# Another written order of all operations for a gated linear attention fused with an expert-style MLP

## The chip, the cores and the metric

One core of a Trainium2 chip runs the whole program. The metric is the device time of one execution in microseconds, and the median of several runs is compared. Profiles are of one execution.

## The reference

For 4 batches of 8 heads, 768 steps and a head width of 40, the first half is a recurrent attention with input, forget and output gates. The second half is an MLP from 320 to 2,048 to 320 on all 3,072 tokens.

```python
for t in range(S):
    m_new = np.maximum(f_gate[:, :, t] + m, i_gate[:, :, t])
    f_stab = np.exp(f_gate[:, :, t] + m - m_new)
    i_stab = np.exp(i_gate[:, :, t] - m_new)
    C = f_stab * C + i_stab * outer(vt, kt)
    n = f_stab * n + i_stab * kt
    y[:, :, t] = sigmoid(o_gate) * (C @ qt) / np.maximum(np.abs(n @ qt), 1.0)
x = y.transpose(0, 2, 1, 3).reshape(B * S, H * D)
h = x @ w_in
sp = np.maximum(h, 0.0) + np.log1p(np.exp(-np.abs(h)))
out = (h * erf(sp)) @ w_out
```

## The kernel before, in words

The sequence is cut into 12 chunks of 64 steps (`NC`), and within a chunk everything is done for two pairs of batches (`r` = 0, 1). A chunk of attention consists of a gate block for every second chunk (`gate_block`: the scan at L303 and what follows to L327), decay factors (`dm`: for chunks 0 and 1 by a matmul at L444 from the tiles `lt`, L340, and `xd`, L350 and L348, with an exponential at L449; later through DRAM, L456), scores on TensorE (L507), the masked product on VectorE (L562), the state and key products (L516, L521) and the value matmuls (L530), the normalisation (L593 to L607) and the state update (L614, L616). The result is transposed on TensorE (L389 to L393) and split into a rounded half and a remainder, `xh` (L402, ACT) and `xl` (L406, VectorE).

The weights of the MLP arrive as 64-bit words whose two 32-bit halves are put together on the core: L624 and L635 on VectorE, L630 on ACT. Those of `w_in` are then split into halves `wh` (L645, L683, ACT) and `wl` (L649, L687, VectorE). They come in four parts of 512 columns.

The MLP of a chunk has 4 groups (`mlp(g)`, 48 in all), each of 512 of the 2,048 middle columns. A group's first matmuls (L748) write two or four `h` tiles, for which PSUM has two buffers. ACT empties them (L759). Then follow softplus (L768), erf (L772), the product (L776), a split (L786 or L788 and L792), and the output matmuls (L812 for the first four groups, L814 to L817 for the others). Exponential, softplus and erf lie in three different tables of ACT, and a change of table is an instruction of its own (L876).

Every piece is added to a plan with its engine and its dependencies. Nothing decides the order at run time: `ORDER`, a list of 1,595 numbers, gives the order in which all operations are written, and each engine, SP's DMA queue included, works through its own in that order. A negative number -n writes n filler matmuls (L873), which compute nothing and keep TensorE busy during the start. A table load is written wherever the next ACT operation needs another table than the one loaded.

```python
for i in order:
    if i < 0:
        stay(-i)
        continue
    o = self.ops[i]
    if o.table and loaded not in o.table:
        loaded = o.table[0]
        load(loaded)
    o.fn()
```

Of the kernel before, what the change touches and what calls it, by code (L numbers as in the profile page):

```python
# [33 lines left out]
class Plan:  # L34
# [60 lines left out]
    1, 4, 0, 3, 5, 7, 9, 11, 12, 6, 13, 2, 14, 15, 16, 8, 17, 33, 27, 32, 34, 36, 35, 20, 19, 31, 38, -1, 40, 28, 26, 29, 93,  # L95
    95, 349, 350, 351, 42, -2, 47, 94, 48, 49, 18, 67, 68, 99, 96, 10, 50, 59, 60, 25, 37, 30, 39, 52, 65, 23, 100, 101, 102,
    105, 107, 106, 108, 41, -2, 55, 44, 66, 72, 56, 109, 43, 24, 71, 354, 45, 46, 111, 112, 57, 74, 76, 58, 22, 69, 73, -1, 64,
    75, 70, 103, 104, 352, 353, 357, 97, 98, 51, 53, 135, 136, 137, 138, 63, 139, 110, 54, 140, 129, 130, 131, 132, 21, 169,
    171, 170, 133, 172, 61, 163, 358, 78, 83, 134, 86, 164, 84, 85, 221, 222, 165, 166, 62, 241, 157, 173, 174, 167, 168, 159,
    239, 240, 125, 127, 158, 160, 175, 199, 200, 161, 242, 88, 193, 77, 91, 201, 195, 205, 207, 223, 224, 225, 162, 273, 79,  # L100
    80, 81, 82, 87, 89, 274, 202, 203, 355, 371, 206, 141, 194, 142, 121, 92, 122, 275, 276, 90, 248, 226, 489, 208, 490, 491,
    204, 196, 249, 227, 356, 369, 113, 209, 250, 143, 197, 251, 361, 114, 372, 210, 115, 494, 149, 126, 128, 492, 457, 467,
    374, 198, 286, 287, 150, 123, 288, 373, 376, 230, 362, 363, 289, 176, 299, 493, 151, 231, 458, 459, 462, 124, 152, 495,
    117, 211, 116, 300, 118, 375, 119, 290, 252, 232, 243, 244, 380, 316, 317, 333, 120, 228, 366, 468, 370, 377, 291, 719,
    720, 378, 382, 212, 359, 364, 365, 721, 185, 384, 360, 496, 253, 145, 379, 392, 337, 233, 245, 389, 186, 724, 466, 368,
    146, 381, 177, 178, 153, 318, 154, 189, 229, 383, 190, 390, 391, 456, 394, 144, 301, 469, 472, 367, 191, 155, 147, 148,
    156, 246, 187, 385, 386, 387, 388, 460, 292, 498, 192, 397, 398, 188, 267, 319, 347, 217, 455, 218, 234, 343, 725, 393,
    395, 396, 268, 461, 474, 320, 277, 302, 235, 247, 181, 497, 399, 400, 278, 464, 475, 473, 236, 477, 465, 470, 334, 182,
    471, 981, 425, 479, 481, 482, 426, 213, 484, 321, 322, 219, 293, 261, 501, 401, 179, 605, 726, 511, 294, 254, 502, 402,
    427, 428, 183, 214, 595, 728, 303, 429, 215, 512, 265, 476, 438, 439, 478, 220, 412, 279, 184, 180, 266, 323, 259, 463,  # L110
    257, 335, 503, 271, 263, 280, 480, 488, 510, 485, 593, 509, 606, 258, 486, 237, 238, 216, 260, 324, 729, 264, 336, 487,
    499, 722, 504, 727, 262, 483, 338, 596, 272, 255, 256, 297, 430, 723, 513, 269, 270, 281, 516, 345, 304, 982, 305, 983,
    505, 295, 298, 500, 296, 325, 339, 340, 326, 327, 597, 440, 506, 431, 508, 986, 413, 306, 307, 329, 330, 414, 331, 519,
    284, 432, 403, 328, 514, 741, 525, 527, 532, 529, 282, 283, 530, 521, 522, 594, 515, 308, 309, 518, 285, 520, 441, 442,
    415, 416, 417, 418, 443, 341, 1243, 603, 523, 344, 524, 742, 312, 313, 310, 404, 405, 348, 526, 550, 551, 406, 576, 990,
    311, 528, 577, 314, 537, 538, 419, 598, 315, 407, 517, 507, 563, 564, 408, 731, 433, 533, 444, 536, 342, 1244, 531, 599,
    608, 740, 552, 553, 554, 607, 539, 540, 565, 732, 534, 535, 1245, 600, 602, 743, 746, 613, 615, 578, 420, 409, 619, 621,
    410, 411, 346, 421, 730, 604, 609, 626, 610, 623, 624, 601, 616, 612, 423, 541, 542, 445, 625, 543, 555, 566, 857, 858,
    859, 614, 617, 618, 611, 620, 424, 436, 579, 631, 632, 633, 640, 641, 642, 733, 736, 622, 634, 635, 630, 636, 652, 653,
    654, 984, 985, 1248, 673, 674, 675, 655, 748, 422, 656, 657, 734, 735, 446, 661, 662, 663, 739, 862, 679, 680, 681, 627,  # L120
    628, 434, 694, 695, 738, 696, 332, 1249, 867, 682, 683, 684, 437, 556, 637, 638, 639, 697, 698, 567, 749, 751, 699, 544,
    700, 701, 755, 658, 659, 660, 580, 664, 702, 545, 629, 451, 452, 453, 744, 745, 987, 703, 676, 435, 677, 678, 685, 752,
    757, 759, 762, 760, 643, 686, 447, 548, 549, 448, 557, 449, 750, 753, 754, 704, 705, 756, 546, 547, 788, 568, 569, 581,
    789, 790, 558, 570, 791, 792, 793, 559, 737, 761, 830, 831, 665, 832, 582, 836, 837, 838, 758, 571, 855, 839, 840, 841,
    687, 561, 809, 815, 562, 574, 988, 989, 810, 816, 811, 644, 450, 767, 868, 869, 872, 768, 817, 860, 861, 856, 766, 666,
    797, 747, 798, 560, 572, 769, 1246, 818, 819, 645, 646, 573, 763, 866, 874, 799, 864, 820, 1247, 764, 765, 873, 776, 777,
    778, 1003, 770, 771, 772, 647, 875, 583, 881, 1004, 1005, 584, 870, 1002, 1119, 575, 794, 795, 773, 774, 796, 775, 667,
    706, 877, 589, 833, 812, 590, 993, 994, 688, 834, 591, 454, 585, 586, 883, 587, 800, 835, 842, 813, 865, 650, 651, 671,
    888, 707, 843, 885, 886, 878, 814, 588, 648, 871, 1129, 1130, 863, 876, 879, 1120, 880, 649, 669, 991, 821, 914, 668, 670,
    690, 779, 689, 915, 916, 882, 708, 1131, 1134, 917, 918, 919, 935, 936, 937, 801, 672, 893, 894, 895, 709, 691, 938, 939,  # L130
    710, 940, 692, 693, 992, 592, 941, 715, 716, 780, 781, 802, 884, 956, 822, 995, 1008, 942, 943, 1010, 962, 887, 892, 957,
    958, 711, 782, 963, 964, 823, 920, 921, 922, 902, 903, 717, 1121, 712, 904, 889, 944, 945, 783, 946, 899, 786, 996, 997,
    900, 901, 1006, 713, 998, 824, 1000, 890, 1001, 896, 1250, 1255, 897, 898, 844, 803, 923, 924, 925, 947, 926, 804, 1128,
    1251, 1011, 825, 1017, 1256, 1007, 965, 966, 959, 960, 961, 891, 784, 1019, 1024, 1021, 1257, 1013, 905, 787, 785, 807,
    808, 1260, 805, 967, 968, 1014, 1022, 948, 1012, 999, 1015, 1016, 828, 1009, 927, 906, 806, 949, 1092, 1093, 1094, 1029,
    845, 829, 1030, 1031, 928, 1095, 1096, 1097, 826, 1018, 950, 951, 1050, 1098, 1020, 1051, 1099, 1052, 1100, 846, 714, 1252,
    1122, 907, 1035, 1036, 1037, 1025, 1026, 1028, 1038, 1039, 1135, 969, 1040, 1118, 1127, 1136, 1117, 1123, 851, 718, 1264,
    1265, 1056, 1124, 1126, 1381, 1057, 1058, 827, 847, 1053, 1054, 1055, 848, 849, 1059, 1060, 1061, 1023, 1101, 1102, 1103,
    929, 852, 970, 1382, 1032, 1125, 1071, 853, 1072, 1073, 1137, 930, 1143, 908, 1033, 1034, 1077, 909, 971, 1078, 1079, 1062,
    1063, 910, 1080, 1139, 1074, 1081, 912, 1027, 1145, 1253, 1147, 1150, 1148, 1140, 1075, 1076, 913, 1132, 1133, 1082, 1268,  # L140
    1254, 933, 934, 911, 954, 1138, 1104, 1105, 1106, 1141, 1142, 1064, 1083, 1041, 1144, 854, 972, 955, 977, 1262, 1149, 1176,
    1177, 1042, 1178, 931, 932, 1218, 1146, 1151, 1219, 1220, 1084, 978, 979, 1263, 980, 1224, 1225, 1226, 1043, 1155, 1156,
    952, 1197, 1157, 1065, 1198, 1152, 1199, 1044, 953, 1185, 1186, 1164, 1154, 1187, 1266, 1267, 1270, 1165, 1166, 973, 1383,
    1045, 974, 975, 1107, 1221, 1222, 1258, 1223, 1161, 1162, 1271, 1048, 1259, 1163, 1390, 1391, 1085, 1269, 1182, 1183, 1200,
    1201, 1184, 1202, 1066, 1153, 1273, 1158, 1159, 1160, 1227, 1228, 1229, 1049, 1275, 1276, 1179, 1180, 1086, 1279, 1181,
    1392, 1395, 1206, 1108, 1069, 1389, 976, 1203, 1167, 1207, 1204, 1070, 1379, 1281, 1286, 1283, 1188, 1189, 1046, 1047,
    1067, 1090, 1208, 1205, 1284, 1272, 1274, 1277, 1068, 1088, 1393, 1380, 1278, 1333, 1334, 1354, 1355, 1087, 1089, 1335,
    1280, 1357, 1358, 1261, 1387, 1356, 1359, 1291, 1292, 1293, 1282, 1287, 1288, 1388, 1360, 1361, 1168, 1362, 1290, 1339,
# [789 lines left out]
```

## Time and profile before

| | |
|---|---|
| median of 3 runs | 459.67 us (459.19 to 460.89) |
| span of the profiled execution | 456.7 us |
| TensorE busy | 445.6 us, 98% of the span |
| VectorE busy | 336.5 us, 74% |
| ACT busy | 328.5 us, 72% |
| mean granted TensorE clock | 0.996 |
| moved by DMA | 51.82 MB, mean 113 GB/s |

The span runs from the first to the last instruction of the profiled execution; a run's time has what lies around it too, so the two differ by some 3 us. Matmuls are pipelined and their ends are modelled, so a TensorE that is busy for a whole stretch is one that was never seen without a matmul under way. The profile lists a full float32 matmul twice. "Idle before" is the time that an engine stood still ahead of an instruction, with the one that ended the wait.

### The profile page before, as it was taken

How to read it: one execution, taken by the hardware profiler on the slowest of the kernel's cores; microseconds unless marked ns; L12 is line 12 of the kernel's file. 1: busy time of each engine (PE TensorE's matmuls, PEld its weight loads, DVE VectorE, ACT ScalarE, POOL GpSimd, SP SyncE). 2: the span in 40 equal slices, each digit the busy share in tenths (PEclk: the TensorE clock that was granted, in tenths of full speed). 3: DMA queues.
4: the chain of work that ended last, by engine and by line, in shares of the span. 5: the costliest groups of instructions: out<-in, count | busy, mean ns of one | idle time of the engine just before them, and what ended most of it. 6: DMA issues, size and time to landing. Idle time of an engine off the chain costs nothing.

```text
span 456.7 us, 14133 instructions
## 1 busy us (share of the span) xinstructions
PE 445.6 (98%) x6118; PEld 401.6 (88%) x6118; DVE 336.5 (74%) x657; ACT 328.5 (72%) x524; POOL 37.3 (8%) x62
## 2 busy tenths in 40 slices
PE   6979999999999999999999999999999999999996
PEld 4569988888999988989998998899898899999996
DVE  5899989799768766588468948776845869548762
ACT  4758999898976946855996984998445584773760
POOL 2000131003300220001021100001110000000000
PEclk9989999999999999999999999999999999999999
DMA  7889696836613430065405217342341100100011
GB/s 273 273 264 332 170 321 177 217 95 199 184 40 106 136 107 3 3 195 130 133 1 163 72 27 238 72 113 78 107 128 26 30 1 2 29 2 15 1 45 29
DMA packets 46831, 51.82 MB, mean 113 GB/s; under 512 B 27056, under 2 KB 31664, under 8 KB 46768
## 3 DMA queue, kind: packets, MB, share of 16 engines
q1 hardware_dynamic: 46768, 50.91, 38.2%
q8 instruction: 48, 0.79, 0.7%
q14 instruction: 15, 0.12, 0.1%
HBM read 46.77 MB, written 4.13 MB: 111 GB/s over the span
## 4 chain that ended last, share of the span: by engine, by line
PE 92%; DVE 3%; ACT 2%; DMA 1%; issue 1%; SPq 0%; DVEq 0%
PE h L748 40%; PE pob L816 11%; PE pob L814 11%; PE pob L817 11%; PE pa L530 3%; PE pa L507 3%; PE pa L516 3%; PE pa L812 2%; PE pob L812 2%; PE pa L521 2%; PE pa L389 2%; PE pa L444 1%; PE pob L873 1%; DMA eT<-gd 1%; DMA gt<-in_gates_dram 1%
## 5 line engine op out<-in xcount | busy, mean ns | idle before, releaser
L748 PE MATMUL h<-xh,wh 128*128 128x256 f32 (+1 forms) x768 | 201.4, 345 | 0.2 <-DVE hb L764 0.2
L748 PEld LDWEIGHTS h<-xh,wh 128*128 128x128 f32 x768 | 126.0, 190 | 14.1 <-DVE hb L764 0.5
L759 ACT ACTIVATE hb<-h 128x256 f32<-128x256 f32 (+1 forms) x160 | 66.7, 422 | 82.7 <-PE h L748 82.6
L748 PE MATMUL h<-xh,wl 128*128 128x256 f32 x384 | 108.5, 283 | 0.2 <-DVE wl L649 0.2
L816 PE MATMUL pob<-woh,gh 128*128 128x320 f32 x336 | 101.1, 313 | 0.0
L817 PE MATMUL pob<-wo,gh 128*128 128x320 f32 x336 | 100.1, 310 | 0.0
L764 DVE TENSOR_TENSOR hb<-h,hb 128x256 f32<-128x256 f32 x128 | 53.1, 420 | 45.8 <-ACT hb L759 45.2
L748 PEld LDWEIGHTS h<-xh,wl 128*128 128x128 f32 x384 | 72.9, 190 | 2.7 <-DVE wl L649 0.5
L876 ACT ACT_TABLE_LOAD x54 | 69.3, 1283 | 1.7 <-PEq L926 0.8
L776 DVE TENSOR_TENSOR n<-n,hb 128x1024 f32<-128x1024 f32 x48 | 58.6, 1227 | 14.8 <-ACT n L772 14.7
L817 PEld LDWEIGHTS pob<-wo,gh 128*128 128x128 f32 x336 | 63.2, 188 | 1.4
L816 PEld LDWEIGHTS pob<-woh,gh 128*128 128x128 f32 x336 | 63.2, 188 | 0.5
L814 PE MATMUL pob<-woh,gl 128*128 128x320 f32 x336 | 62.7, 312 | 0.0
L485 POOL TENSOR_SCALAR_AFFINE_SELECT dm<-dm 128x512 f32<-128x512 f32 (+1 forms) x40 | 34.0, 856 | 293.9 <-ACT dm L465 256.6
L792 DVE TENSOR_TENSOR gl<-n,gh 128x1024 fp32r<-128x1024 f32 x44 | 53.9, 1228 | 2.2 <-ACT gh L786 1.9
L814 PEld LDWEIGHTS pob<-woh,gl 128*128 128x128 f32 x336 | 53.5, 188 | 2.0
L768 ACT ACTIVATE n<-hb 128x1024 f32<-128x1024 f32 x48 | 49.3, 1058 | 1.6 <-DVE hb L764 1.3
L772 ACT ACTIVATE n<-n 128x1024 f32<-128x1024 f32 x48 | 49.6, 1054 | 0.2
L786 ACT ACTIVATE gh<-n 128x1024 fp32r<-128x1024 f32 x28 | 29.5, 1052 | 0.0
L406 DVE TENSOR_TENSOR xh<-pa,xh 128x384 fp32r<-128x384 f32 x24 | 13.3, 554 | 15.1 <-ACT xh L402 15.1
L562 DVE TENSOR_TENSOR dm<-pa,dm 128x512 f32<-128x512 f32 x24 | 16.5, 687 | 9.6 <-ACT xh L402 6.0
L530 PEld LDWEIGHTS pa<-kvo,dm 64*32 64x32 f32 x1536 | 16.7, 106 | 5.9 <-issue 5.0
(99 smaller groups left out, 469.6 us busy)
## 6 DMA issues: line engine op xcount, KB each, us to landing
qk<-in_qk_dram SPq DMA_DIRECT2D x24, 512.0 KB
kvo<-in_kvo_dram SPq DMA_DIRECT2D x24, 484.0 KB
eT<-gd SPq DMA_DIRECT2D x44, 128.0 KB
raw<-in_w_out_dram SPq DMA_DIRECT2D x16, 320.0 KB
dm<-gd SPq DMA_DIRECT2D x40, 128.0 KB
raw<-in_w_in_dram SPq DMA_DIRECT2D x8, 512.0 KB
out_dram<-o SPq DMA_DIRECT2D x48, 80.0 KB
raw<-in_w_in_dram SPq DMA_DIRECT2D x4, 256.0 KB
```

What stands on the lines that cost most here:

```text
L485: nc.gpsimd.affine_select(out=x, in_=x, pattern=[[0, H], [1, L]], compare_op=ALU.is_ge, fill=0.0, base=base, channel_multiplier=-1)
L748: nc.tensor.matmul(h[:, n * T:n * T + n_], w, m, start=(s == 0), stop=(s == len(ops) - 1))
L759: nc.scalar.activation(part(), G(f'h{i}')[:, T:2 * T] if wide else G(f'h{i}'), AF.Copy)
L764: nc.vector.tensor_tensor(part(), G(f'h{i}')[:, 0:T], part(), op=ALU.add)
L768: nc.scalar.activation(new('n0', [128, 1024], ('n0', g)), G('hb'), AF.Softplus)
L772: nc.scalar.activation(G('n0'), G('n0'), AF.Erf)
L776: nc.vector.tensor_tensor(G('n0'), G('n0'), G('hb'), op=ALU.mult)
L792: nc.vector.tensor_tensor(new('gl', [128, 1024], ('gl', g), F32R), G('n0'), G('gh').bitcast(F32), op=ALU.subtract)
L814: nc.tensor.matmul(acc(b), G('gl')[:, ts], woh[:, j], start=False, stop=(j == NFF - 1))
L816: nc.tensor.matmul(acc(b), G('gh')[:, ts], woh[:, j], start=(j == 0), stop=False)
L817: nc.tensor.matmul(acc(b), G('gh')[:, ts], t['wol', j], start=False, stop=False)
L876: plan.run(ORDER, lambda k: nc.scalar.preload_act_table_set(KIND[k]), stay)
```

## The change

The list `ORDER` is replaced by another permutation of the same operations. No operation, tile or buffer count is touched, and six filler matmuls are written in both, at other places.

```diff
 ORDER = [
-    1, 4, 0, 3, 5, 7, 9, 11, 12, 6, 13, 2, 14, 15, 16, 8, 17, 33, 27, 32, 34, 36, 35, 20, 19, 31, 38, -1, 40, 28, 26, 29, 93,
...
+    4, 135, 9, -2, 0, 12, 137, 5, 99, 8, 6, -1, 136, 2, 1, 3, -1, 138, 11, 7, 13, 139, 32, 31, 101, 14, 105, 15, 17, 349,
...
```

What it does is seen on the queues. First SP's DMA queue at the start of the program (`cst` are the constants, `gt` the gates, `raw` weights, `kvo` and `qk` the attention's inputs), before:

```order
L223 DMA cst<-in_consts_dram 128x12
L293 DMA gt<-in_gates_dram 128x2x128
L439 DMA kvo<-in_kvo_dram 128x968
L435 DMA qk<-in_qk_dram 128x2x512
L439 DMA kvo<-in_kvo_dram 128x968
L657 DMA raw<-in_w_in_dram 128x1024
```

and in the changed kernel:

```order
L657 DMA raw<-in_w_in_dram 128x1024
L223 DMA cst<-in_consts_dram 128x12
L293 DMA gt<-in_gates_dram 128x2x128
L657 DMA raw<-in_w_in_dram 128x1024
L439 DMA kvo<-in_kvo_dram 128x968
L435 DMA qk<-in_qk_dram 128x2x512
L673 DMA raw<-in_w_in_dram 64x1024 x2
```

Two blocks of first-layer weights and the tail block now stand among the first transfers, one of them ahead of the constants.

Second, VectorE at the start, up to the gate scan (L303), as the difference of the two:

```order
 L934 UNCONDITIONAL_BRANCH
+L272 MEMSET state_71 128x328
 L252 TENSOR_TENSOR sel<-cst 128x1
 L253 TENSOR_TENSOR sel<-cst 128x1
 L254 TENSOR_TENSOR sel<-sel 128x1
 L255 TENSOR_SCALAR sel<-sel 128x1
-L272 MEMSET state_71 128x328
+L268 TENSOR_SCALAR heads_of<-cst,sel 128x8
 L259 TENSOR_SCALAR sel<-block,sel 128x4
+L624 TENSOR_SCALAR raw<-raw 128x512
+L635 SCALAR_TENSOR_TENSOR raw<-raw 128x512
 L303 SCALAR_TENSOR_TENSOR m<-gt,m 128x128
```

The decoding of the first weight block now stands ahead of the gate scan, and the head mask (`heads_of`) moves ahead of it as well.

Third, TensorE ahead of the first expert matmul (L748; `pa` are the attention's tiles in PSUM, `pob` the fillers'). Before, this stands there, and behind its last row nine more of the same value block (L521 and L530) and then L748:

```order
L507 MATMUL pa<-qk 64x64 x32
L873 MATMUL pob_77<-ident 128x512
L360 MATMUL pa<-ident,x 128x32 x2
L389 MATMUL pa<-ident,kvo 128x128 x2
L392 MATMUL pa<-ident,kvo 64x128
L393 MATMUL pa<-ident,kvo 64x128
L516 MATMUL pa<-state_72,qe 64x41 x16
```

and in the changed kernel:

```order
L530 MATMUL pa<-kvo,dm 32x41 x32
L873 MATMUL pob_77<-ident 128x512 x2
L389 MATMUL pa<-ident,kvo 128x128 x2
L392 MATMUL pa<-ident,kvo 64x128
L393 MATMUL pa<-ident,kvo 64x128
L389 MATMUL pa<-ident,kvo 128x128 x2
L392 MATMUL pa<-ident,kvo 64x128
L393 MATMUL pa<-ident,kvo 64x128
L507 MATMUL pa<-qk 64x64 x16
L360 MATMUL pa<-ident,x 128x32 x2
L748 MATMUL h<-xh,wh 128x256 x2
```

One of chunk 1's two score blocks and its first state and value block (L516, L521, L530) now stand behind the first expert matmuls. Further on, all engines' rows are shuffled in the same way, and ACT has 66 table loads (L876) where it had 54.

## Rows read from the trace of the kernel before

**Rows 1.** The page's first part: busy us (share of the span) xinstructions of each engine.
```profile
PE 445.6 (98%) x6118; PEld 401.6 (88%) x6118; DVE 336.5 (74%) x657; ACT 328.5 (72%) x524; POOL 37.3 (8%) x62
```

**Rows 2.** Table by stretches: length; busy (x) of PE, PEld, DVE, ACT, POOL; PEclk, DMA share, GB/s.
```profile
core 0: us, PE busy (x) PEld busy (x) DVE busy (x) ACT busy (x) POOL busy (x), PEclk, DMA share, GB/s
...
10.00:20.00 10.00, 9.85 (x272) 5.80 (x273) 8.03 (x22) 7.73 (x23) 0.00 (x0) 1.00 1.03 340
20.00:30.00 10.00, 7.23 (x194) 4.65 (x196) 9.50 (x20) 6.61 (x14) 0.00 (x0) 1.00 0.73 202
30.00:40.00 10.00, 9.77 (x155) 9.00 (x158) 9.49 (x21) 6.08 (x11) 0.00 (x0) 0.83 1.03 333
...
140.00:160.00 20.00, 20.00 (x378) 19.28 (x377) 15.58 (x34) 17.60 (x25) 2.71 (x4) 1.00 0.43 123
160.00:180.00 20.00, 20.00 (x262) 17.61 (x261) 11.95 (x26) 10.02 (x22) 2.71 (x4) 1.00 0.20 63
```

**Rows 3.** Timeline, 27 to 41 us, PE and DVE: start, length, engine, line, operation.
```profile
27.47 0.65 PE L530 MATMUL pa<-kvo,dm 64*32 64x41 f32 x46
...
29.34 0.56 DVE L406 TENSOR_TENSOR xh<-pa,xh 128x384 fp32r<-128x384 f32 x1
...
29.95 0.38 PE L530 MATMUL pa<-kvo,dm 64*32 64x41 f32 x18 [1.83 <-issue]
...
30.26 0.51 PE L748 MATMUL h<-xh,wh 128*128 128x256 f32 x2
...
33.89 0.58 PE L748 MATMUL h<-xh,wl 128*128 128x256 f32 x1 [0.23 <-DVE wl L649]
...
38.73 0.68 PE L516 MATMUL pa<-state,qe 40*64 40x41 f32 x32
...
40.53 0.51 PE L748 MATMUL h<-xh,wh 128*128 128x256 f32 x2
```

**Rows 4.** Timeline, 0 to 20 us, the same columns.
```profile
0.80 0.40 SPq L223 DMA_DIRECT2D cst<-in_consts_dram  x1
...
2.55 0.16 DVE L252 TENSOR_TENSOR sel<-cst 128x1 f32<-128x1 f32 x1 [2.55 <-DMA cst<-in_consts_dram]
...
3.90 0.48 DVE L303 TENSOR_TENSOR_SCAN m<-gt,m 128x128 f32<-128x128 f32 x1 [0.32 <-DMA gt<-in_gates_dram]
...
6.72 1.06 ACT L340 ACTIVATE lt<-x,sel 128x64 f32<-128x64 f32 x4 [2.54 <-DVE x L327]
...
7.18 0.69 DVE L350 TENSOR_TENSOR xd<-x,heads_of 128x512 f32<-128x512 f32 x1
...
8.02 1.96 PE L444 MATMUL pa<-xd,lt 128*128 128x512 f32 x4
...
9.15 0.60 ACT L449 ACTIVATE dm<-pa 128x512 f32<-128x512 f32 x1 [1.37 <-PE pa L444]
...
10.21 2.00 ACT L348 ACTIVATE xd<-x,heads_of 128x64 f32<-128x64 f32 x8
...
19.07 0.81 PE L530 MATMUL pa<-kvo,dm 64*32 64x41 f32 x64
```

**Rows 5.** VectorE's groups by form: busy us, mean ns of one, idle before.
```profile
L562 DVE TENSOR_TENSOR dm<-pa,dm 128x512 f32<-128x512 f32 x24 | 16.5, 687 | 9.6 <-ACT xh L402 6.0
...
L478 DVE TENSOR_TENSOR qe<-qk,eT 104x512 f32<-104x512 f32 x22 | 16.0, 725 | 0.0
...
L635 DVE SCALAR_TENSOR_TENSOR raw<-raw 128x512 int32<-128x512 int32 x10 | 6.9, 690 | 0.6
...
L649 DVE TENSOR_TENSOR wl<-raw,wh 128x512 fp32r<-128x512 f32 x8 | 5.5, 682 | 0.5 <-ACT wh L645 0.5
...
L624 DVE TENSOR_SCALAR raw<-raw 128x512 int32<-128x512 int32 x10 | 4.2, 422 | 0.0
...
L687 DVE TENSOR_TENSOR wh<-raw,wh 64x512 fp32r<-64x512 f32 x4 | 2.7, 687 | 0.1
```

**Rows 6.** The chain that ended last, one group of sixteen L748.
```profile
82.83 1.91 PE h L748 x16
```

**Rows 7.** ACT's groups: table loads, busy us, mean ns of one, idle before.
```profile
L876 ACT ACT_TABLE_LOAD x54 | 69.3, 1283 | 1.7 <-PEq L926 0.8
```

140 rows, old and new, of the table ORDER are left out of this document.

## The prediction, made before the changed kernel was run

> **What bounds the kernel now.** Read the busy shares first: TensorE is busy for 445.6 of 456.7 us [rows 1], so only some 11 us of the span can be won without shortening its work, and the change shortens none of it. The table by stretches says where the 11 us lie. TensorE is busy for 9.85 of the ten microseconds from 10 to 20, for 7.23 from 20 to 30 and 9.77 from 30 to 40, there with a granted clock of 0.83, and from 140 on for 20.00 of 20 [rows 2]. From about 34 us to the last matmul the kernel is a TensorE queue that never runs dry, and any order that keeps it fed ends when the work ends. What an order can still change is how early the queue fills, and whether it runs dry later.
>
> The timeline shows how it fills. The first expert matmul (L748) starts at 30.26. Before it the queue waits 1.83 us inside the value matmuls of chunk 1, which the profile puts down to issue, but VectorE's last half of the activations (L406) ends at 29.90, so without that wait the first expert matmul would have waited for VectorE to about the same moment [rows 3]. Three microseconds on, a matmul waits for a weight half (L649, at 33.89) [rows 3]. VectorE is busy for 9.50 of 10 us from 20 to 30 and 9.49 from 30 to 40 [rows 2]. So the start is bound by VectorE's queue and by the order in which inputs land, and everything after it by TensorE.
>
> **The change, part by part.** All 1,595 operations stay, as do the six filler matmuls; three things move.
>
> *Constants behind a weight block.* The first transfer is now 512 KB of w_in. The constants were issued at 0.80 and were there at 2.55 [rows 4]. At the 340 GB/s of the busy stretch [rows 2] the block takes 1.54 us. If the constants queue fully behind it they come 1.54 late, if they run beside it, not at all; I take 1.2, nearer to the queue, since the sixteen DMA engines are fully busy at that rate (share 1.03 [rows 2]): 3.75. Ahead of the gate scan (L303, 3.90 before [rows 4]) VectorE now also decodes that block: L624 0.42 and L635 0.69 [rows 5]. The scan starts at about 3.75 + 1.1 for the small constants + 1.1 = 5.95, 2.05 later. The head mask, once between scan and decay factors (about 0.3 us), now stands ahead, so the decay factors (L350, 7.18 before) come 1.75 late at 8.95, and the first decay matmul (8.02 before [rows 4]) at 9.8.
>
> *ACT's own queue.* Two blocks of L340 (1.06 each [rows 4]) and the 0.3 us exponential now stand ahead of the first decay exponential (9.15 before): it runs from 11.2 to 11.8, 2.05 late [rows 4]. Scores then run to 12.55, and the first value matmuls end near 14.2, about 1.2 late. From there the new order gains: the second half of ACT's decay factors (2.00 us, [rows 4]) ends at 14.5, the scores of the second pair wait for VectorE to free their buffer (gate block 2.3, one L624 0.42, normalisation 1.0 after 13.35, so 17.3), and its value matmuls run at about 19.7 against 19.07 before [rows 4]. That leaves the start 0.6 us late, not early.
>
> *What stands ahead of the first expert matmul.* Before, both score blocks of chunk 1 and one whole value block stood there, and on VectorE the operations that go with them. Now one score block does. VectorE after the normalisation (22.2) has two halves, two weight pieces and a decode between: L649, L687, L635, L406, L624, L406, 3.6 us, to 25.85. The first expert matmul then starts at about 26.4, 3.85 us earlier than 30.26. TensorE has done less by then: a value block with its state product (38.73 to 40.53, 1.80 us [rows 3]) and a score block (0.65). Net: +1.4 us.
>
> *The next VectorE point.* The value block of chunk 1's first pair now needs VectorE's L562 24 instructions later. Those are four L635, three L624 and two each of L649, L687, L478 and L562, 9.6 us by their means [rows 5], and nine of 0.2 to 0.5, 3.5 us: 13.1. At the pace of 30 to 40 us (21 in 9.49 us [rows 2]) 24 take 10.8. I take 12.8, nearer to the sum of the forms, because these are the long ones. So 38.65, with small waits 38.85, and the block ends at 39.65. TensorE, with two 1.91 us groups [rows 6], the other block and two groups more, would be there at 37.6 and waits. Before, the same block ended at 40.53 [rows 3], with one 1.91 us group fewer and one set of transposes (0.78) more done. Gain: 0.88 + 1.91 - 0.78 = **2.0 us**. Ends: if VectorE keeps the faster pace and the constants do not queue, TensorE sets the end here and the gain is about 4.5; if the clock falls as before and VectorE is held up by it, 0.5.
>
> *Twelve more table loads.* ACT's order holds 66 where 54 stood, at 1,283 ns [rows 7]: 15.4 us of ACT. ACT is busy for 328.5 of 456.7 us [rows 1], so the cover is its own idle time of 128 us, and the sum takes nothing. The worst stretch is from the first group of experts of chunk 3 to the last of chunk 5 (about 120 to 200 us), where 13 loads stand instead of 7. From 140 to 180 ACT is busy for 17.60 and 10.02 of 20 [rows 2], 12.4 us idle against 7.7 us of added loads. If that cover were gone, each load would cost TensorE up to 1.283 us, because only two PSUM buffers hold its results until ACT has emptied them.
> What a load costs is shown by its row: 1,283 ns, and 1.7 us of idle time ahead of all 54 together [rows 7]. The Trainium skill (ScalarE: Activation LUTs, What ACT_TABLE_LOAD costs) adds a drain of about 1,380 ns to every switch, 2.66 us in all; by it the added loads would be an estimated 32 us of ACT, and six of them 16 us, more than the idle time of 140 to 180. By that rule the trace disagrees: no such drain stands beside the loads here as idle time.
>
> **Sum.** 456.7 - 2.0 = 454.7 us of span. The median of the runs, 459.67, lies 3.0 above that span, which I take as unchanged: **457.7 us**, 0.43% faster. A measurement of this kernel can tell about 0.5%, 2.3 us, from no change.
>
> **The rivals.**
> *The gain is larger.* VectorE is not the limit at the value block, and the clock never falls. For it: two stretches with TensorE's loss, 2.77 us from 20 to 30 and some 1.7 from the clock [rows 2], need not come again. Against it: VectorE is already busy for 9.5 of 10 there, and the new order asks 24 of its instructions first. Gain 4.5: 455.2.
> *The clock takes it back.* The new order leaves TensorE little to do from 14.2 to 17.4, with one decay matmul between. Before, the granted clock of 30 to 40 was 0.83, that is 3.4 of the ten microseconds at 1.2 GHz and 1.7 us lost, after the wait that ended at 29.95 [rows 2, 3]. If it drops at the new gap, score and value blocks and the two fillers that stand ahead of the transposes run at 1.2 GHz and all that follows is late by about 1.7 us: 459.4.
> *Slower: the loads starve TensorE.* Place: 120 to 200 us, six added loads. It decides once four of the added loads fall where ACT has no idle time: 5.1 us, more than the 2.0 won and the 2.3 of the measurement. For it: two result buffers only, and ACT's share in that stretch goes to about 90%. Against it: from 160 to 180 ACT is idle half the time, and in the crowded stretches of the kernel before TensorE still never stopped. 457.7 + 5.1: 462.8.
> *It is no different.* That the table changes nothing is excluded, since the rows of every queue move; that the start only changes places, with the first weights early and the gates late, is the lower end of the forecast.
>
> **How the numbers follow.** Forecast 0.50, spread from 456.3 to 458.9, with 0.4 of it past the 0.5% line at 457.4; larger gain 0.20; clock 0.20, inside the line; loads 0.10, of which 0.02 stay inside it. Faster: 0.20 + 0.20 = 0.40. Slower: 0.08. Within: 0.52. The range runs from the larger gain, 455.2, to a drop of the clock with one uncovered load besides, 459.4 + 1.0 = 460.4; the loads and the far end of the larger gain are left out.
>
> **What would show it.** Right: the first L748 at 26 to 27 us, the constants at 3.3 to 4.1, a TensorE wait of about a microsecond for L562 before the value block at 39, TensorE at 20.00 of 20 from 60 us on, 66 loads, and the last matmul near 450.3. Wrong: a first L748 after 28.5, a granted clock below 1 between 15 and 30, L759 with its two buffers as what TensorE waits for between 120 and 200, or a wait between the last expert group and the last output matmuls, where 60 matmuls now stand and 72 did. A first L748 before 25 would speak for the larger gain.

## The result, and the profile after

The changed kernel took 465.35 us (median of 20 runs, 460.01 to 467.58), the kernel before 459.88 (20 runs, 458.25 to 462.51): a ratio of 1.0092, 95% interval 1.0067 to 1.0117. The ratio leaves out the three slowest of the twenty runs, which count as slow; the quotient of the two medians over all runs is 1.0119. The forecast of 457.7 is wrong in sign, and 465.35 lies beyond its range, which ended at 460.4. The profiled execution after took 461.46 us with a span of 459.7, so it is one of the faster ones: sixteen of the twenty runs took longer than 463 us. A second profile (464.19 us) follows below.

From the page of the changed kernel, the busy shares and ScalarE's table loads:

```profile
PE 446.5 (97%) x6118; PEld 401.9 (87%) x6118; DVE 333.1 (72%) x657; ACT 344.1 (75%) x536; POOL 37.9 (8%) x62
...
L876 ACT ACT_TABLE_LOAD x66 | 84.7, 1283 | 1.9 <-PEq L926 0.8
```

Against [rows 1] and [rows 7], TensorE's work is the same to 0.9 us, and the twelve added loads stand there with 15.4 us of ScalarE and 1.9 us of idle time ahead of all 66 together. The span is 3.0 us longer, so TensorE stands or is slowed somewhere. The table by stretches of the changed kernel (columns as in [rows 2]) says where:

```profile
10.00:20.00 10.00, 6.82 (x155) 3.87 (x159) 7.47 (x20) 8.06 (x25) 0.00 (x0) 0.83 0.97 251
20.00:30.00 10.00, 9.16 (x187) 6.01 (x177) 8.82 (x19) 5.96 (x11) 0.00 (x0) 1.00 0.95 274
30.00:40.00 10.00, 9.31 (x217) 8.61 (x218) 9.32 (x21) 7.67 (x13) 0.00 (x0) 1.00 0.99 293
70.00:80.00 10.00, 9.79 (x162) 6.97 (x162) 9.40 (x23) 9.94 (x17) 1.37 (x2) 1.00 0.70 199
80.00:90.00 10.00, 8.60 (x142) 7.28 (x140) 4.49 (x10) 7.01 (x10) 0.00 (x0) 1.00 0.86 223
90.00:100.00 10.00, 9.59 (x169) 9.23 (x170) 7.82 (x15) 7.83 (x16) 1.47 (x3) 0.83 0.90 255
...
140.00:160.00 20.00, 20.00 (x384) 19.34 (x383) 17.37 (x36) 18.02 (x26) 1.75 (x2) 1.00 0.35 95
160.00:180.00 20.00, 20.00 (x185) 18.49 (x184) 13.87 (x25) 16.75 (x26) 1.31 (x2) 1.00 0.42 119
```

Two places stand out. From 10 to 20 us TensorE has 6.82 us of work instead of 9.85 [rows 2], though it regains some from 20 to 30. And from 70 to 100 us, where the kernel before shows 10.00 of 10 in each stretch, it is idle for 0.21, 1.40 and 0.41 us, and the granted clock in the last is 0.83. From 140 on, where the loads were expected to bite if anywhere, it is at 20.00 of 20.

The start, in the timeline of the changed kernel (columns as in [rows 3]):

```profile
1.26 0.42 SPq L223 DMA_DIRECT2D cst<-in_consts_dram  x1
...
4.90 0.16 DVE L252 TENSOR_TENSOR sel<-cst 128x1 f32<-128x1 f32 x1 [3.63 <-DMA cst<-in_consts_dram]
...
7.08 0.48 DVE L303 TENSOR_TENSOR_SCAN m<-gt,m 128x128 f32<-128x128 f32 x1
...
9.02 0.57 SPq L293 DMA_DIRECT2D gt<-in_gates_dram  x1
...
11.00 2.85 PE L444 MATMUL pa<-xd,lt 128*128 128x512 f32 x4 [1.94 <-ACT lt L340]
...
15.95 0.48 DVE L303 TENSOR_TENSOR_SCAN m<-gt,m 128x128 f32<-128x128 f32 x1 [0.22 <-DMA gt<-in_gates_dram]
...
19.67 0.69 PE L507 MATMUL pa<-qk 40*64 40x64 f32 x32 [2.07 <-DVE kvo L601]
...
21.94 0.81 PE L530 MATMUL pa<-kvo,dm 64*32 64x41 f32 x64
...
28.39 0.48 PE L748 MATMUL h<-xh,wh 128*128 128x256 f32 x2
...
40.99 0.81 PE L530 MATMUL pa<-kvo,dm 64*32 64x41 f32 x64
41.73 0.44 PE L389 MATMUL pa<-ident,kvo 128*128 128x128 f32 x2
```

The constants are used at 4.90 (2.55 before [rows 4]), the first scan starts at 7.08 (3.90 [rows 4]). The second block of gates has one buffer, so it can be asked for only when the first scan's chain is done, at 9.02 (5.92 before); its scan runs at 15.95 (11.34 before), and it stands on VectorE ahead of the normalisation (L601) for which the second pair's scores wait 2.07 us. The first expert matmul still comes 1.87 us earlier than before [rows 3], but it has less behind it.

The second place, in the same timeline:

```profile
78.93 0.38 SPq L435 DMA_DIRECT2D qk<-in_qk_dram  x1
...
86.89 0.69 DVE L478 TENSOR_TENSOR qe<-qk,eT 104x512 f32<-104x512 f32 x1 [3.01 <-DMA qk<-in_qk_dram]
...
87.73 0.68 PE L516 MATMUL pa<-state,qe 40*64 40x41 f32 x32 [0.75 <-DVE qe L478]
...
88.82 1.06 ACT L786 ACTIVATE gh<-n 128x1024 fp32r<-128x1024 f32 x1 [2.56 <-DVE n L776]
...
90.41 0.76 PE L748 MATMUL h<-xh,wh 128*128 128x256 f32 x2 [1.06 <-ACT hb L759]
```

VectorE waits 3.01 us for the query and key block of chunk 3, asked for at 78.93 (74.67 before). Its product L776, which makes the input of the output matmuls, is queued behind that wait, ScalarE's L786 behind the product, ScalarE's emptying of a result buffer (L759) behind that, and TensorE waits 1.06 us for the buffer. The clock then falls.

### The profile page after: what moved, and what is told of

Its sections match the earlier page's. It is cut to its first block, busy times and chain, and to the rows that moved or that the text cites. A ratio compares the mean times of both kernels' runs of the same rounds, so it can differ in the third digit from the quotient of the medians.

```text
span 459.7 us, 14174 instructions
## 1 busy us (share of the span) xinstructions
PE 446.5 (97%) x6118; PEld 401.9 (87%) x6118; DVE 333.1 (72%) x657; ACT 344.1 (75%) x536; POOL 37.9 (8%) x62
## 4 chain that ended last, share of the span: by engine, by line
PE 83%; DVE 8%; DMA 5%; issue 2%; ACT 1%; SPq 0%; DVEq 0%; ACTq 0%
PE h L748 35%; PE pob L814 11%; PE pob L816 11%; PE pob L817 11%; PE pa L530 4%; DMA qk<-in_qk_dram 3%; PE pa L516 3%; PE pa L507 2%; PE pa L812 2%; PE pa L521 2%; DMA gt<-in_gates_dram 2%; PE pa L389 1%; DVE raw L624 1%; DVE wo L635 1%; DMA cst<-in_consts_dram 1%
## 5 line engine op out<-in xcount | busy, mean ns | idle before, releaser
L748 PE MATMUL h<-xh,wh 128*128 128x256 f32 (+1 forms) x768 | 202.7, 344 | 1.1 <-ACT hb L759 1.1
L748 PEld LDWEIGHTS h<-xh,wh 128*128 128x128 f32 x768 | 126.9, 190 | 14.2 <-ACT hb L759 1.2
L759 ACT ACTIVATE hb<-h 128x256 f32<-128x256 f32 (+1 forms) x160 | 65.7, 421 | 61.7 <-PE h L748 61.4
L748 PE MATMUL h<-xh,wl 128*128 128x256 f32 x384 | 108.3, 282 | 0.0
L817 PE MATMUL pob<-wo,gh 128*128 128x320 f32 x336 | 99.8, 309 | 0.0
L876 ACT ACT_TABLE_LOAD x66 | 84.7, 1283 | 1.9 <-PEq L926 0.8
L748 PEld LDWEIGHTS h<-xh,wl 128*128 128x128 f32 x384 | 72.9, 190 | 1.8
L776 DVE TENSOR_TENSOR n<-n,hb 128x1024 f32<-128x1024 f32 x48 | 58.9, 1231 | 10.2 <-ACT n L772 10.2
L817 PEld LDWEIGHTS pob<-wo,gh 128*128 128x128 f32 x336 | 63.1, 188 | 1.6
L814 PE MATMUL pob<-woh,gl 128*128 128x320 f32 x336 | 63.5, 313 | 0.0
L814 PEld LDWEIGHTS pob<-woh,gl 128*128 128x128 f32 x336 | 53.4, 188 | 2.5
L786 ACT ACTIVATE gh<-n 128x1024 fp32r<-128x1024 f32 x28 | 29.4, 1053 | 4.7 <-DVE n L776 3.9
L562 DVE TENSOR_TENSOR dm<-pa,dm 128x512 f32<-128x512 f32 x24 | 16.5, 687 | 14.1 <-PE pa L507 11.0
L822 ACT ACTIVATE o<-pob 128x320 f32<-128x320 f32 x22 | 9.5, 432 | 17.6 <-PE pob L814 17.6
L530 PEld LDWEIGHTS pa<-kvo,dm 64*32 64x32 f32 x1536 | 16.8, 106 | 5.2 <-issue 4.4
```

Of the source, the lines that this page charges most:

```text
L530: nc.tensor.matmul(y[os, j, p], w[ds, j, p, ts], v[ds, 2 * p + j], start=False, stop=(p == NPR - 1))
L748: nc.tensor.matmul(h[:, n * T:n * T + n_], w, m, start=(s == 0), stop=(s == len(ops) - 1))
L759: nc.scalar.activation(part(), G(f'h{i}')[:, T:2 * T] if wide else G(f'h{i}'), AF.Copy)
L776: nc.vector.tensor_tensor(G('n0'), G('n0'), G('hb'), op=ALU.mult)
L814: nc.tensor.matmul(acc(b), G('gl')[:, ts], woh[:, j], start=False, stop=(j == NFF - 1))
L817: nc.tensor.matmul(acc(b), G('gh')[:, ts], t['wol', j], start=False, stop=False)
```

## The experiments

Three theories. **T1**: transfers behind 45 us come late. **T2**: the twelve added table loads. **T3**: the start.

To compare kernels of different order I use TensorE's *lag*: the start of a matmul less the work that TensorE had done by then, each matmul counted at its usual interval in the steady part (0.117 us for one L748 of 256 columns, 0.147 for one of L814 to L817, and so on; the whole program is 423.8 us). It is worked out from one profile each, while a median is of 5 to 20 runs. The ratios, with their intervals, are those on record against runs of the kernel before taken beside each kernel; they are not quotients of the medians in the table.

| kernel | median | ratio (interval) | lag at 50 us | added 70 to 110 | added 110 to 410 |
|---|---|---|---|---|---|
| before | 459.88 | | 20.1 | 1.3 | 6.3 |
| changed | 465.35 | 1.0092 (1.0067-1.0117) | 20.3 | 4.9 | 5.8 |
| changed, second profile | | | 24.3 | 3.7 | 5.9 |
| e4, before + 12 loads | 473.34 | 1.0294 (1.0264-1.0325) | 19.9 | 1.3 | 19.3 |
| e7, before, weights first | 464.64 | 1.0093 (1.0060-1.0126) | 26.1 | 1.4 | 6.4 |
| e10, new start, old rest | 461.18 | 1.0041 (1.0016-1.0065) | 25.4 | 1.5 | 6.6 |
| e9, old start, new rest | 465.65 | 1.0124 (1.0105-1.0143) | 23.9 | 5.2 | 6.7 |
| e5, constants first | 463.52 | 1.0064 (1.0042-1.0085) | 23.1 | 4.0 | 6.7 |
| e6, scan behind | 463.89 | 1.0073 (1.0045-1.0102) | 24.5 | 6.0 | 6.5 |
| e3, block early | 466.18 | 1.0143 (1.0116-1.0171) | 22.8 | 6.2 | 6.5 |
| e11, three early | 463.71 | 1.0115 (1.0074-1.0155) | 19.6 | 4.8 | 5.9 |
| e13, three early, work behind | 468.18 | 1.0198 (1.0154-1.0242) | 23.8 | 7.7 | 6.2 |
| e12, before, block late | 461.12 | 1.0032 (1.0010-1.0054) | 20.6 | 2.6 | 6.9 |
| e14, six transfers less | 460.96 | 1.0035 (1.0004-1.0066) | 25.5 | 2.1 | 5.7 |
| e15, before, six less | 458.71 | 0.9977 (0.9955-0.9999) | 21.0 | 1.3 | 6.0 |

In e1 to e3 the lines are 4 lower than in the changed kernel, in e4 2 higher, in e14 4 higher from line 696 on. OLD and NEW are the two lists; numbers are operations.

**e1 and e2: halves, joined at 70 us** (the rest in its order as far as the buffers allow).

```diff
-ORDER = NEW
+ORDER = NEW[:327] + [i for i in OLD if i not in NEW[:327]]    # e1
+ORDER = OLD[:316] + [i for i in NEW if i not in OLD[:316]]    # e2
```

> The new order up to its 327th operation (about 70 us), the rest in the order of before; 58 table loads. If the loss comes from the new order of the transfers behind 45 us, of which the query and key block of chunk 3 is the one seen late (T1), this runs like the kernel before, within 0.3%: 458.5 to 461.3 us. If the new start costs, with its constants at 4.9 us and its clock drop at 12 us (T3), it runs as the changed kernel does: 463 to 465 us. The table loads (T2) say 460 to 461.

> The order of before up to its 316th operation (about 70 us), the rest in the new order; 65 table loads. If the transfers behind 70 us cost (T1), 463 to 465 us, and VectorE waits some us for the query and key block of chunk 3 near 87 us. If the start costs (T3), 459.5 to 460.5 us. If the table loads cost (T2), 464 to 465 us.

Measured: 476.48 (ratio 1.0344, 1.0309 to 1.0380) and 467.79 (1.0174, 1.0142 to 1.0206), both beyond every theory. The waits of TensorE from 95 to 110 us in e1 and from 80 to 95 in e2:

```profile
PE h L744 <- ACT xh L398: 10.8, 1, 10.8
```

```profile
PE pa L385 <- DVE state L610: 4.7, 1, 4.7
```

The join itself stalls: at 70 us the two orders have done different operations, and what one has left over is missing for the other. Neither run tells the halves apart.

**e4: twelve more table loads in the kernel before.**

```diff
-                loaded = o.table[0]
+                was, loaded, n = loaded, o.table[0], n + 1
+                if 17 <= n < 29:
+                    load(next(k for k in 'XSG' if k not in (was, loaded)))
                 load(loaded)
```

> The order of before with twelve more table loads on ScalarE, one ahead of each of twelve loads that are there anyway, between 120 and 290 us: 66 loads, 15.4 us more of ScalarE. If loads lie beside TensorE's work (T1, T3), within 0.3% of the kernel before. If they cost (T2), 4 to 15 us more: 464 to 475 us.

Measured: 473.34, 13.5 us more, in the range of T2. Two stretches of e4:

```profile
160.00:170.00 10.00, 8.01 (x194) 6.89 (x193) 4.11 (x8) 7.88 (x12) 0.43 (x1) 1.00 0.22 72
...
240.00:250.00 10.00, 7.56 (x41) 6.28 (x42) 5.21 (x8) 9.92 (x12) 2.25 (x4) 1.00 0.00 0
```

So a load that an order makes no room for costs 1.1 us here (13.5/12), and "beside other work" is no property of loads. But the changed kernel makes the room: with the same 66 loads its lag grows by 5.8 us from 110 to 410 us, against 6.3 before and 19.3 in e4.

**The changed kernel again.**

> The changed kernel once more, for a second profile: its runs lie between 460.0 and 467.6 us, and the profile shown is of 461.5. If the spread comes from the start (T3), a profile near 465 us shows the value matmuls of the second pair waiting more than 2.1 us for the normalisation of VectorE, whose scan waits for the second block of gates, and a clock drop behind it, and TensorE 22 to 25 us behind at 45 us instead of 20.05. If it comes from the stretch between 80 and 110 us (T1), TensorE is 20 us behind at 45 us and over 26 at 110.

Measured: 464.19 us. Both places: TensorE's waits from 10 to 30 us, and two stretches.

```profile
PE pa L507 <- DVE kvo L601: 2.9, 1, 2.9
```

```profile
80.00:90.00 10.00, 10.00 (x53) 7.69 (x52) 5.31 (x15) 9.54 (x14) 0.00 (x0) 1.00 0.98 271
90.00:100.00 10.00, 8.76 (x212) 8.27 (x211) 9.09 (x17) 7.42 (x14) 1.31 (x2) 1.00 0.68 203
```

The wait at the start is 2.9 instead of 2.07, TensorE is 24.3 us behind at 50 instead of 20.3, and from 70 to 110 it loses 3.7 more. The longer wait is only 0.85 of the 4.0 us between the two starts. The rest is the clock, which falls twice before 50 us instead of once, and a wait of 2.0 instead of 0.7 inside the value matmuls.

The start varies in the same way over all profiles that have it unedited. Lag at 50 us and mean granted clock from 0 to 50: 19.6 at 1.00 (e11, below), 20.3 at 0.97 (changed), 22.8 at 0.93 (e3), 23.8 at 0.93 (e13), 24.3 at 0.93 (second profile), 25.4 at 0.90 (e10), 25.5 at 0.90 (e14). With the old start it is 19.9 to 21.0 in four profiles, at 0.97 to 1.00. The lower the clock of the start, the further behind TensorE is, and which is cause and which effect the profiles do not tell. The second place is there each time.

**e7: only the first transfers of the change, in the kernel before.**

```diff
-    1, 4, 0, 3, 5, 7, 9, 11, 12, 6, ..., 31, ...
+    1, 4, 135, 0, 3, 5, 7, 9, 11, 12, 99, 6, ..., 31, 105, ...
```

> The kernel before with three weight blocks asked for among the first transfers as the change does (one ahead of the constants, one behind the gates, one behind the first queries), all else as before. T3: the first scan starts 1.5 to 3 us later and TensorE ends 2 to 4 us later: 461.5 to 464 us. T1: 459.5 to 460.5 us, as the kernel before.

Measured: 464.64, 0.6 above the range of T3. The second block of gates in e7's timeline:

```profile
7.84 0.58 SPq L293 DMA_DIRECT2D gt<-in_gates_dram  x1
...
18.58 0.49 DVE L303 TENSOR_TENSOR_SCAN m<-gt,m 128x128 f32<-128x128 f32 x1 [3.73 <-DMA gt<-in_gates_dram]
```

Three weight blocks asked for early cost 0.93% by themselves in that order; the longest wait that the trace shows for it on VectorE is this one, for the gates that land behind them.

**e5 and e6: the start mended in part.**

```diff
-    4, 135, 9, -2, 0, 12, 137, ...
+    0, 12, 4, 135, 9, -2, 137, ...        # e5
-    350, 106, 47, 59, 35, 351, 48, ..., 49, 29, 107, 30, 67, ...
+    106, 47, 59, 35, 48, ..., 49, 29, 107, 30, 350, 351, 67, ...   # e6
```

> The changed kernel with the constants and the first block of gates asked for first, ahead of the weight block. T3: first scan at about 4.3 us instead of 7.1, second block of gates asked for at about 6.2 instead of 9.0 and landed by 13, no wait of the second pair's value matmuls over 1 us; 1 to 3 us faster than the changed kernel, 461 to 464 us, and a smaller spread. T1: 464 to 466 us.

> The changed kernel with one edit on VectorE alone: the scan of the second block of gates moved behind the normalisation of the first pair, instead of ahead of it. T3: the wait of the second pair's value matmuls (2.1 to 3.5 us in three profiles) falls below 1 us whenever the block lands; the median falls by 1.5 to 3 us, to 462 to 464 us. T1: 464.5 to 466 us.

Measured: 463.52 and 463.89, both inside T3's ranges, 1.8 and 1.5 us under the changed kernel's median, within reach of the intervals. The medians came out as T3 said, but partly by luck, since the mechanisms were only half right. In e5 the constants are there at 2.62, but the scan starts at 7.96: VectorE's decoding of the first weight block stands ahead of it, so asking earlier was no use there, and the second block of gates is asked for at 9.91 instead of the expected 6.2. In e6 the wait falls to 0.9, and a wait of 1.6 for L562 takes its place.

**e9 and e10: halves, joined where both orders have done the same.** After 151 operations of the old order and 156 of the new (about 37 us) they differ in nine.

```diff
+ORDER = OLD[:151] + [i for i in NEW if i not in OLD[:151]]    # e9
+ORDER = NEW[:156] + [i for i in OLD if i not in NEW[:156]]    # e10
```

> The order of before for its first 151 operations (about 37 us), then the new order; at this seam the two orders have done the same operations but for nine, so that nothing is left over to be caught up. If all of the loss arises in the start (T3): 459.5 to 461 us, within 0.3% of the kernel before. If the transfers between 70 and 90 us cost by themselves (T1): TensorE as far behind at 70 us as in the kernel before and 2 to 4 us further at 110 us, 462 to 464 us.

> The new order for its first 156 operations (about 37 us), then the order of before, at the same seam. T3: 463.5 to 465.5 us, as the changed kernel, TensorE 22 to 25 us behind at 45 us. T1: 460 to 461.5 us. If both halves cost, e9 and e10 each lie between the two kernels and their losses add up to about the 5.5 us between the medians.

Measured: e9 465.65, above both ranges; e10 461.18, in the range of T1. The stretches from 80 to 100 us, of e9 and then of e10:

```profile
80.00:90.00 10.00, 10.00 (x56) 7.84 (x55) 4.83 (x13) 9.52 (x13) 0.00 (x0) 1.00 0.99 266
90.00:100.00 10.00, 8.73 (x212) 8.24 (x211) 9.17 (x18) 7.46 (x14) 1.31 (x2) 1.00 0.70 209
```

```profile
80.00:90.00 10.00, 10.00 (x135) 7.84 (x127) 9.56 (x21) 9.01 (x16) 1.07 (x2) 1.00 0.63 171
90.00:100.00 10.00, 10.00 (x257) 9.47 (x257) 7.37 (x14) 8.43 (x13) 0.00 (x0) 1.00 0.74 206
```

The loss from 70 to 110 us belongs to the new rest, whatever start stands before it, and is absent with the old rest even 25 us behind. The new start alone costs 0.41%, 1.9 us, by its median (nine of its twelve runs took 459.2 to 462.1 us, three 463.4 to 465.2; the profile is of one of the three). The halves don't add up to the whole (0.41 + 1.24 against 0.92): in e9 the lag grows by 4.2 us between 35 and 50 us, where the new rest needs weights that only the new start fetches first.

**e3 and e11: transfers of that place asked for earlier.**

```diff
 SP's queue of the changed kernel
+ 455 (queries and keys, chunk 3), ahead of 177                # e3
+ 145, 141 (output weights), 455, ahead of 364 (eT, 62.2 us)   # e11
```

> The new order with one transfer moved: the query and key block of chunk 3 is asked for ahead of the output weights and the tables that stand before it on SyncE's queue. If that block is what costs (T1), the 3.0 us wait of VectorE near 87 us is gone, the clock stays up between 85 and 95 us and the time is 460 to 461.5 us. If it is the table loads (T2) or the start (T3), 464 to 465.5 us as for the changed kernel.

> The changed kernel with three transfers moved on SyncE's queue alone: two blocks of the output weights and the query and key block of chunk 3 are asked for ahead of the two transfers of gate products at 62 us, for which SyncE stands 4.6 us waiting on VectorE's state update. If the stretch from 70 to 110 us is lost to transfers that come late (T1): no wait of VectorE for that block, TensorE falls back by less than 2.5 us between 70 and 110 us instead of 3.7 to 6.2, and the median falls by 1.5 to 3.5 us, to 462 to 464 us. If the order of the engines in that stretch costs by itself: 464.5 to 466 us.

Measured: 466.18 and 463.71 (e11's median is in T1's range, though its ratio, 1.0115, is no better than the changed kernel's, and its interval covers that one); the lag from 70 to 110 us grows by 6.2 and 4.8, as without the edit. T1 in its narrow form, that this one block costs, falls. The waits of VectorE around 90 us, of e3 and of e11:

```profile
DVE raw L620 <- DMA raw<-in_w_out_dram: 3.1, 1, 3.1
```

```profile
DVE raw L624 <- DMA raw<-in_w_out_dram: 2.6, 1, 2.6
```

Another transfer, the output-weight block that lands last, has taken its place in VectorE's queue.

**e13: e11, with that block's preparation moved out of the way too** (206, 207 and 208 behind 236, 261 and 192).

> The kernel of three_early with one more edit: the preparation of the output-weight block that lands last (one operation on ScalarE, two on VectorE) is moved behind the gating of the expert columns that stands after it, so that neither late block stands ahead of work that TensorE waits for. T1 (late transfers, whichever stands first in an engine's queue): VectorE and ScalarE wait for no transfer between 80 and 92 us, TensorE falls back by 1.3 to 2.5 us between 70 and 110 us (4.8 in three_early), the median falls by 1.5 to 3 us below that of the changed kernel, to 462 to 464 us, what is left being the start. If the order of the engines or the table loads of that stretch cost by themselves: it falls back by 3.5 us or more again, with ScalarE busy ahead of the wait.

Measured: 468.18, and a miss: the lag grows by 7.7. From 70 to 100 us it grows by 2.5 (1.3 before), but then the displaced work is in the way, and a third transfer is late. Waits from 84 to 104 us:

```profile
PE pa L516 <- DVE qe L478: 1.8, 1, 1.8
DVE vg L495 <- DMA kvo<-in_kvo_dram: 1.5, 1, 1.5
```

TensorE waits 1.8 us at 102 us, and the granted clock from 100 to 110 is 0.66.

**e12: the kernel before with that block asked for later** (725, 181, 497, 465 and 470 ahead of 455).

> The kernel before with five transfers (a block of output weights, two of gate products, the next query and key block, two of exponentials) asked for ahead of the query and key block of chunk 3 instead of behind it; nothing else is moved. T1: VectorE waits 2 to 5 us for that block near 82 us, TensorE falls back by 2.5 to 5 us between 70 and 110 us instead of 1.3, and the time is 461.5 to 464 us. If late transfers are hidden there: 459.3 to 460.5 us, as before.

Measured: 461.12, 0.3% slower, just under T1's range. The wait, from 78 to 95 us, and the stretch:

```profile
DVE qe L478 <- DMA qk<-in_qk_dram: 2.8, 1, 2.8
```

```profile
80.00:90.00 10.00, 9.04 (x143) 7.47 (x140) 6.79 (x14) 7.48 (x11) 0.00 (x0) 1.00 0.71 208
```

A wait of VectorE of 2.8 us for one transfer costs TensorE 0.96 us there, and 1.5 us in all.

**e14 and e15: six transfers of that place left out, in both kernels.**

```diff
+            same = {6: 5, 11: 4, 8: 15, 13: 5, 14: 4, 12: 15}     # e15: {8: 1, 7: 10, 11: 5, 15: 1, 9: 10, 14: 5}
+            if j in same:
+                t[R] = t['rawo', same[j]]
+                return
             nc.sync.dma_start(new('raw', [128, 1024], R, I32)[:, 0:2 * DM], ...
```

> The changed kernel without six of its transfers: six blocks of output weights that are asked for between 65 and 79 us (1.97 MB) are not loaded, and their preparation works on the buffers of three blocks loaded before (the output therefore leaves these six blocks out); every engine's instructions and their order stay. T1 (the stretch from 70 to 110 us is lost to transfers that come late and to the buffers they wait for): TensorE falls back by 0.5 to 2 us there instead of 3.7 to 6.2, with no wait of VectorE for a transfer over 0.5 us between 80 and 92 us; 461.5 to 463.5 us. If the engines' order or the table loads cost there by themselves: 3.5 us or more again, 464 to 466 us.

> The same control on the kernel before: six blocks of output weights that are asked for between 60 and 84 us are not loaded (the output leaves them out). If nothing waits for transfers in this stretch of the kernel before, it falls back by 1.3 us from 70 to 110 us as it does now, and the time is within 0.3% of the kernel before (T1 and its rival alike); a gain over 1 us would say that late transfers cost there too.

Measured: e14 460.96, 4.4 us under the changed kernel by the medians (2.6 by the ratios) and below T1's range, though the lag from 70 to 110 us still grows by 2.1; e15 458.71, 0.9 under the kernel before in the same runs (459.57). The stretches of e14:

```profile
80.00:90.00 10.00, 10.00 (x125) 7.58 (x116) 8.05 (x19) 9.59 (x16) 0.00 (x0) 1.00 0.76 227
90.00:100.00 10.00, 10.00 (x224) 9.61 (x223) 8.32 (x18) 8.61 (x15) 1.31 (x2) 1.00 0.58 184
100.00:110.00 10.00, 10.00 (x203) 8.39 (x203) 7.57 (x15) 9.89 (x15) 1.31 (x2) 1.00 0.44 108
```

With the engines' order unchanged and ScalarE at 9.59 and 9.89 of 10, TensorE never stops from 80 to 110 us, and from 70 to 110 the lag grows by 0.8 us more than in the kernel before instead of 2.4 to 4.9 more. So what stopped TensorE there is not the engines' order or the loads by themselves, but the transfers and the buffers that they wait for; the run does not separate these two. Its price is less certain: e14 gains 0.57% on the changed kernel, of which e15 has 0.23% as well, and the 0.34% between them (1.6 us) is not clear of the intervals. The bytes agree: by 80 us the kernel before had moved 20.7 MB and the changed one 19.7, with TensorE equally far (lags of 21.3 and 21.6). One place where they fall behind is SP's queue, which works in its written order: from 57.3 to 62.2 us it stands 4.6 us before an `eT` whose buffer waits for VectorE's state update, and the DMA engines have a share of 0.62 from 60 to 70 us, against 0.89 in the kernel before. That this stall is what makes the later transfers late is not shown: in e11 three of them were asked for ahead of it, and the lag grew all the same.

## Why the prediction was wrong

Two steps of the prediction failed.

*What bounds the kernel.* "From about 34 us to the last matmul the kernel is a TensorE queue that never runs dry" was read from the kernel before and then taken to hold for the new order. **This is the first step that failed.** The prediction walked SP's queue through the first microseconds only, and asked of the later part whether ScalarE had time, not when its inputs land. It had no term for transfers behind 45 us. The runs show TensorE idle for 2.0 us from 70 to 100 us, gone from 80 to 110 when six transfers are left out. That removal gives back 0.57% by the ratios (1.0092 against 1.0035), 2.6 us, of which 0.23% is also had in the kernel before.

*The start.* **The second step that failed is the gain of 2.0 us**, the whole of the forecast sum. The runs show a loss instead: 1.9 us by the median of e10. The terms that make it up follow.

*Constants behind a weight block.* Forecast 3.75, measured 4.90: 2.35 us late instead of 1.2, more than the bound for queueing fully behind one block (1.54). They were asked for 0.46 us later as well, behind that block. The scan came at 7.08 instead of 5.95, the first decay matmul at 11.00 instead of 9.8: the error is 1.1 to 1.2 there.

*ACT's own queue.* "Its value matmuls run at about 19.7 ... the start 0.6 us late." They ran at 21.94, 2.9 late. Two things that the sum had no term for hold VectorE here. The second block of gates could not be asked for before the first chain had freed its buffer, and its scan ran at 15.95 and 15.93 in the two profiles. And in the first profile the clock fell at 12.0 us, in the midst of the decay matmuls: they took 2.85 us instead of 1.96 [rows 4], so that VectorE was busy with what follows them until just before the gates landed, and waited 0.22 us for them; in the second, at full clock, it waited 1.09.

*The first expert matmul.* Forecast 26.4, measured 28.39: later by about what had been lost ahead of it.

*The gain of 2.0 us.* Not there. VectorE's pace was right (24 instructions in 12.5 us, forecast 12.8), but they start 2.0 late, and TensorE did not wait for the last of them. The value block ended at 41.73 instead of 39.65, and with that the prediction's own sum gives 40.53 - 41.73 + 1.91 - 0.78, or -0.1 us. The lag at 50 us says the same of this execution, 20.3 against 20.1. It is one of the best of the seven starts (19.6 to 25.5); the middle one is at 23.8, and the new start alone is 1.9 us slower by its median (e10). The terms ahead were mis-sized, all in the same direction, and the falls of the clock come on top.

*Twelve more loads at nothing.* Right for this order, as far as the lag tells (lag from 110 to 410: 5.8 against 6.3; e14, with all 66, 5.7). The rival price, up to 1.283 us for a load without cover, is about what e4 measured, 1.1.

*The clock.* The rival allowed for one fall, worth 1.7 us. Its place was right: in the profiled execution the granted clock falls at 12 us, after TensorE's wait of 1.94 us, and once more at 90.5 behind its wait for L759. Its sum was too small: in the second profile it falls between 20 and 25 us (0.66) and again from 37.7 to 41.1, and over the seven starts TensorE is at 1.2 GHz for none of the first 50 us up to 10 of them (mean clock 1.00 to 0.90).

*The median 3.0 us above the span, "which I take as unchanged".* A run's time is 1.7 to 1.8 us longer than its own span in every run on record, and not some 3. The rest is which execution was profiled: before, one some 1.3 us faster than the median, now one 3.9 us faster, which makes 5.7. So the median and the profile describe different executions. The changed kernel's runs spread over 7.6 us: those with a mean clock of 0.996 took 460.01 to 461.94, those of 0.989 or less 463.99 to 467.58, but those between (0.991 to 0.993) cover 461.46 to 467.15, so the clock is not all of it. The 0.83 from 90 to 100 us is 3.4 us at 1.2 GHz, which loses up to 1.7.

Together: the new start costs 1.9 us (e10), the late transfers 1.6 to 2.6 (e14, with and without what the same removal gives the kernel before), of 4.2 by the ratio. The intervals, 1.1 us and more to either side of each, are too wide to say whether anything else is left. Which of the late transfers matters is not settled by moving single ones (e3, e11, e13), since each time the next one was seen. No version found here beats the kernel before by more than the measurement can tell.

## What to carry to other kernels

When an order is replaced, walk the transfer queue through the whole program, not only through the start: for every block, when it can be asked for (its buffer, and what stands ahead of it), when it lands, and what is queued behind its first reader. A saturated engine in the old profile says that the old order kept it fed, not that the next one will. And join two orders only where both have done the same work; otherwise the seam is what is measured. Last, before a profile is set beside a median, see which of the executions was profiled: here one start gave lags from 19.6 to 25.5 us.

## What the runs showed of the hardware

Asking for a small transfer first brings nothing if its reader is queued behind the reader of a large one (e5: constants there 2.3 us earlier, the scan 0.9 later). A late transfer of 2.8 us before VectorE cost TensorE 0.96 us of idle time (e12), and one of 3.0 us in the changed kernel was followed by waits of TensorE of 0.75 and 1.06 us, and then by a clock of 0.83 from 90 to 100 us. A table load of 1,283 ns cost 1.1 us where the order had no room for it (e4), and nothing measurable where it had (lag from 110 to 410 us: 5.8 against 6.3). One and the same start, in seven profiles, had a mean granted clock of 0.90 to 1.00 over its first 50 us and left TensorE 19.6 to 25.5 us behind.
